# Lead growth over 36 steps, VectorE halves kept away from the sums of a, and h behind one eviction: a planner's rules changed in an attention-then-SwiGLU kernel

## The chip, the cores and the metric

The kernel runs on one core of a Trainium2 chip. The metric is device time in microseconds (us), the median of several runs. One profiled execution gives all rows that are quoted. Engines are named as the profile names them: PE (matrix multiplies; PEld is its weight loads), DVE (VectorE), ACT (ScalarE), POOL (GpSimd), SP (which issues the DMAs).

## The reference, cut to what matters

The input x has 4 batches of 12416 rows of 128 numbers. 32 inducing vectors attend to x and give h, the rows of x attend to h, and every resulting row goes through a gated feed-forward layer of width 1536.

```python
def mab(q, kv):
    s = scale * (q @ kv.transpose(0, 2, 1))
    a = np.exp(s - s.max(-1, keepdims=True))
    a /= a.sum(-1, keepdims=True) + 1e-09
    return a @ kv
h = mab(I, x)                  # (4, 32, 128)
x = mab(x, h)                  # (4, 12416, 128)
g = x @ w_gate; val = x @ w_val
out = (g / (1 + np.exp(-g)) * val) @ w_out
```

## The kernel before, in words

**What is multiplied.** Of each batch the second attention gives a (12416 x 32) only. The product of h with the gate and value weights is formed once a batch, so the feed-forward layer starts from a: its "stack" holds a in two parts (a_hi and a_lo, each 32 rows deep, stacked to a depth of 128). A batch's columns are cut in 25 pieces (COLS) of 512 or 480 rows of x, and each piece passes through 12 tiles of the width 1536: 300 slots a batch.

**One step of the wide part.** From the 13th piece of batch 0 on, two tiles go together (a pair, two slots). `fronts` (L910) issues four matmuls, the gates g of both tiles and the values v of both tiles. `gates` (L920) puts g through Silu on ACT. `values` (L927) forms h from v and the Silu on DVE. `splits` rounds h to fp16 (h_hi, a cast on ACT, L935) and subtracts (h_lo, on POOL, L937). `back` issues three matmuls for each tile (L954, L955, L956) into an accumulator o that gathers 12 tiles (t = 0 to 11). After t = 11 `evac` (L964) moves it out on DVE. `splits` of a pair is issued one pair later than its `values`.

**The lead.** Between `fronts` and `back` of a tile lie several other tiles, the lead (`ahead`, L1067): 8 tiles, and up to 14 while the next batch's first attention is being prepared. It grows by size / RAMP a slot, where size is 2 in the wide part and RAMP is 6, so by 6 tiles in 18 slots; while it grows, some pairs issue the backs of one tile only. At two places a batch, the bursts (the exponentials of the next batch's two attentions, here called e1 and e2), ACT has other work for long, and the lead falls back to 8: PE runs many backs at once.

**PSUM.** Six of the eight banks are three tiles of two banks (ps_two): g of a pair takes one, v the next, in turn. So g of a pair gets the tile that held v of the pair two before, which `values` must have read; v gets that of g of the pair before, which `gates` must have read. The other two banks are ps_o: the accumulator o, and whatever else needs a bank: the sums for the next batch's h (`hacc`, L442), its turning (`h_c`, L508), score visits, and the halves below.

**VectorE's halves.** Where `owned` (L972) says so, a pair is "own": DVE forms its h in two calls, one of them into a ps_o bank, and DVE itself casts and subtracts this half (L935 and L937 with o as operand), so that ACT and POOL have half the work on that pair. 130 of 522 pairs are own. Each needs one of the two ps_o banks until DVE's subtraction, so the next accumulator may have to wait for it.

**What sets the order.** The order on every engine is the order in which the kernel issues. Each batch has a list of steps with due slots (`plan`, `post`), which are issued between the tiles. `post` turns the raw exponentials into a piece of the stack: `sum2` (sum over the 32, two reductions on DVE), `rec2` (reciprocal), `scale2` (ACT), `norm2` (POOL), `aT` (a transpose on DVE), `a_hi` (DVE), `a_lo` (POOL). Steps with `acc` need a ps_o bank and are put off while the oldest waiting tile has t = 11, 0 or 1.

Of the kernel before, what the change touches and what calls it, by code (L numbers as in the profile page):

```python
# [38 lines left out]
NT = DFF // P  # L39
# [7 lines left out]
RAMP = 6  # L47
# [16 lines left out]
OWN = range(1, 7)  # L64
# [48 lines left out]
def induced_set_attention_then_swiglu(ctx: ExitStack, tc: tile.TileContext, xt, xn, ind, wgv, wo, out):  # L113
# [183 lines left out]
        nc.vector.tensor_reduce(out=pair[:, :, 0], in_=in_, op=ALU.add, axis=AX.X)  # L297
        nc.vector.tensor_reduce(out=out, in_=pair, op=ALU.add, axis=AX.X)

    keep = []  # L300

    class Batch:
        pass
# [1 line left out]
    def attention(b, one, xn0=None, xt0=None):  # L305
# [128 lines left out]
        def hacc(q, group):  # L434

            n0, n1 = CH0[group[0]], CH0[group[1]] + CH[group[1]]
            if q == group[0]:
                st.hps = ps_o.tile([P, 512], F32, name="o")
            for i in range(CH[q]):
                tb = CH0[q] + i - n0  # L440
                g = tb % NG
                nc.tensor.matmul(  # L442
                    out=st.hps[32 * g:32 * g + 32, 0:C], lhsT=st.eT[q][:, 32 * i:32 * i + 32], rhs=st.xn[q][:, i, :],
                    start=(tb < NG), stop=(tb >= n1 - n0 - NG))
            if q == group[1] and group[1] < NCH - 1:
                if group[0] == 0:
                    st.hn = att.tile([P, C], F32, name="hn")
                    nc.vector.tensor_copy(out=st.hn, in_=st.hps[:, 0:C])
                else:
                    nc.vector.tensor_add(out=st.hn, in0=st.hn, in1=st.hps[:, 0:C])  # L450

        def h_a():
            ps = bank()
# [6 lines left out]

        def h_b():
            nc.vector.tensor_add(out=st.hn, in0=st.hn, in1=st.hps[:, 0:C])
            nc.vector.tensor_scalar(out=st.hn, in0=st.hn, scalar1=st.r, scalar2=None, op0=ALU.mult)


# [253 lines left out]
    def post(st, q, eng, base, ready=0):  # L719

        f = st.f
        at = (1, 6, 7, 11, 13, 15, 18) if f["half"](q) else (1, 2, 2, 5, 7, 9, 12)
        steps = [(0, lambda: f["sum2"](q)), (at[0], lambda: f["rec2"](q)), (at[1], lambda: f["scale2"](q)), (at[2], lambda: f["norm2"](q, eng)),
                 (at[3], lambda: f["aT"](q)), (at[4], lambda: f["a_hi"](q)), (at[5], lambda: f["a_lo"](q, eng))]
        tiles = [u for u, (p, j) in enumerate(COLS) if p == q]
        return [(base + d, g) for d, g in steps] + [
            (max(base + at[6], ready + NT * (u - NST + 1) + 3), lambda u=u: f["spread"](u)) for u in tiles]
# [76 lines left out]
    with tc.tile_pool(name="xt0", bufs=NCH - NXT) as xt0, tc.tile_pool(name="xn0", bufs=NCH - NXN) as xn0:  # L804
        cur = attention(0, one, xn0, xt0)
        f = cur.f
# [16 lines left out]
        def run(token):  # L823
# [17 lines left out]
            at=f["aT"], ah=lambda q, e=0: f["a_hi"](q, (f["same"], nc.scalar.copy)[e]),  # L841
# [75 lines left out]
    def gates(u):  # L917
        u.s = twin(sip.tile([P, 2 * WF], F32, name="silu"), u)
        for f in halves if u.last else whole:
            nc.scalar.activation(out=f(u.s), in_=f(u.g), func=AF.Silu, scale=u.st.g)  # L920

    def values(u):
        u.h = twin(hp.tile([P, 2 * WF], F32, name="h"), u)
        u.x = ps_o.tile([P, 512], F32, name="o")[:, :u.n] if u.own else None
        u.parts = [(f, u.x if u.own and f is halves[1] else f(u.h)) for f in (halves if u.own else whole)]
        for f, h in u.parts:
            nc.vector.scalar_tensor_tensor(out=h, in0=f(u.v), scalar=u.st.k, in1=f(u.s), op0=ALU.mult, op1=ALU.mult)  # L927
# [13 lines left out]
    acc = {}  # L941
# [28 lines left out]
    quiet = {"own": 0, "step": 0}  # L970

    def owned(slot, burst):  # L972

        soon = [f for a in (cur, nxt) if a is not None for at, f in a.steps if at <= slot + 5]
        ok = not burst and pend and pend[0].t in OWN and slot >= max(quiet.values()) and not any(hasattr(f, "acc") and f.acc for f in soon)
        if ok:
            quiet["own"] = slot + 2 * REST
        return ok

    def parts(u):  # L980
        (splits if u.half else split)(u)

    pend, wait = [], []
# [13 lines left out]
    ahead = len(pend)  # L997
    for b in range(B):
        nxt = attention(b + 1, (one, oneb)[(b + 1) % 2]) if b + 1 < B else None
        if nxt is not None:  # L1000
            nxt.steps = plan(nxt, PA if b == 0 else PB, b + 1)
            if b == 0:
                cur.steps.append((nxt.e1, lambda: run(f"e2:52:{NTB}")))
                for q in range(2, NF):
                    base = NT * (1 + NG * (q - 1) - NST) + 2
                    base = max(base, E0 + 4) if q < 4 else max(base, nxt.e1 + 1)
                    cur.steps += post(cur, q, nc.gpsimd, base)
                cur.steps += [(14 + 6 * i, lambda i=i: peak_of(0, i)) for i in range(6)]
                cur.steps += [(66 + 6 * i, lambda i=i: peak_of(1, i)) for i in range(3)]
                small = [lambda f=f, k=k: f(k) for k in range(2) for f in (peak_a, peak_m, peak_b)] + [peak_c, peak_d]  # L1010
                sizes = [cur.f["size_" + k] for k in "abcdu"]
                small[2].acc = small[5].acc = sizes[1].acc = (NT - 1, 0, 1)
                cur.steps += list(zip((48, 53, 58, 84, 88, 94, 98, 101), small)) + list(zip((62, 68, 78, 82, 108), sizes)) + [(97, cur.f["proj_rounds"])]
                for k in range(2 * NG * NG):
                    cur.steps.append((100 + k // 2, lambda k=k: cur.f["proj_spread"](k // (NG * NG), k // NG % NG, k % NG)))
                cur.steps += [(106 + 6 * i, lambda i=i: (half_a, half_b, half_c)[i % 3](i // 3)) for i in range(9)]
                cur.steps.sort(key=lambda x: x[0])
        bursts = (nxt.bursts if nxt is not None else set()) | ({E0} if b == 0 else set())
        last_burst = max(bursts, default=0)
        slot2 = NT if b == 0 else 0  # L1020
        while slot2 < SLOTS:
            turn = b == 0 and slot2 == NT * CSW
            if turn:
                single.close()
                ps_two = ctx.enter_context(tc.tile_pool(name="ps_two", bufs=3, space=bass.MemoryType.PSUM))
            size = 1 if ps_two is None else 2
            top_, low_ = ((HI, SKEW), (HI2, SKEW2))[size - 1]
            c, t = slot2 // NT, slot2 % NT
            slots = range(slot2, slot2 + size)
            burst = any(x in bursts for x in slots)  # L1030
            if size == 1:
                u = front(cur, b, c, t)
                u.us = [u]
                u.last = False
                u.cast_dve = burst or t in CAST
                gate(u)
                value(u)
            else:
                if turn:
                    back(pend.pop(0))  # L1040
                u = fronts(cur, b, c, t)
                u.last = b == B - 1 and slot2 == SLOTS - 2
                u.cast_dve = burst
                u.own = u.last or owned(slot2, burst)
                gates(u)
                values(u)
            if wait:
                parts(wait[0])
                pend += wait.pop(0).us
            wait.append(u)  # L1050
            if burst:
                parts(u)
                pend += wait.pop(0).us
            def steps(slot):
                for a in (cur, nxt):
                    while a is not None and a.steps and a.steps[0][0] <= slot:

                        if pend and pend[0].t in getattr(a.steps[0][1], "acc", ()):
                            break
                        if getattr(a.steps[0][1], "acc", ()):  # L1060
                            quiet["step"] = slot + 8
                        a.steps.pop(0)[1]()

            for slot in slots:
                if size == 1:
                    steps(slot)
                ahead = min(ahead + size / RAMP, top_) if nxt is not None and slot < last_burst else max(ahead - 1 / RAMP, low_)  # L1067
                if slot in bursts:
                    ahead = low_ - (size == 1)
                while len(pend) + sum(len(x.us) for x in wait) > ahead + (slot != slots[-1]):  # L1070
                    back(pend.pop(0))
                if size == 2:
                    steps(slot)
            slot2 += size
        quiet = {k: at - SLOTS for k, at in quiet.items()}
        if nxt is not None:
            nxt.steps = [(at - SLOTS, f) for at, f in nxt.steps]
        cur = nxt
# [42 lines left out]
```

## Time and profile before

| what | value |
|---|---|
| median of 3 runs | 1409.54 us (1409.5 to 1410.22) |
| the profiled execution's own time | 1409.94 us |
| its span in the trace | 1408.1 us |
| granted PE clock | 0.999 |
| busy share of the span | PE 99%, ACT 86%, POOL 84%, DVE 83% |

Matmuls are pipelined: a row's duration has a tail that lies over the next matmul. The time a matmul takes from PE is the distance from its start to the next one's start, and a wait shows as a longer distance. The idle time that a row prints in brackets is what is left after the tail, some 0.16 us less than the time lost.

### The profile page before, as it was taken

Reading aid. Unit: us, or ns where it says so; the run is one execution under the profiler, and the core shown is the slowest. Engines: PE = TensorE matmul, PEld = TensorE weight load, DVE = VectorE, ACT = ScalarE, POOL = GpSimd, SP = SyncE. Lnnn points to the kernel's source line nnn. Section 1 sums busy time; section 2 is a strip of 40 time slices with the busy share of each in tenths; the row PEclk is TensorE's granted clock in tenths of the full one; section 3 lists DMA queues with packets and bytes.
Section 4 is the critical chain, followed back from the end, with each engine's and each line's share of the span. In section 5 each row is a group of like instructions: output and inputs, shape, how many; then the busy total and the mean of one; then the engine's idle time right before and its main releaser. Section 6 shows DMA issues by size and latency. Waiting matters only on the chain.

```text
span 1408.1 us, 21950 instructions
## 1 busy us (share of the span) xinstructions
PE 1388.9 (99%) x7480; PEld 706.4 (50%) x7480; DVE 1174.0 (83%) x1639; ACT 1209.3 (86%) x1481; POOL 1182.8 (84%) x748
## 2 busy tenths in 40 slices
PE   8999999999999999999999999999999999999998
PEld 6577687444444454444444444444444444444444
DVE  6889878879888777888898777779888889889887
ACT  4988798888898898888889888888888888888887
POOL 1679778998898888988889888988889888888887
PEclk9999999999999999999999999999999999999999
DMA  9224433211132432110103323211011010010010
GB/s 374 75 76 148 166 100 108 99 34 45 32 102 85 163 126 86 46 51 29 32 29 115 138 98 130 100 39 46 24 36 33 31 34 27 31 37 29 22 35 29
DMA packets 52335, 107.03 MB, mean 76 GB/s; under 512 B 13440, under 2 KB 34432, under 8 KB 52224
## 3 DMA queue, kind: packets, MB, share of 16 engines
q1 hardware_dynamic: 52224, 105.64, 22.2%
q8 instruction: 59, 0.97, 0.3%
q14 instruction: 52, 0.43, 0.1%
HBM read 62.87 MB, written 25.43 MB: 63 GB/s over the span
## 4 chain that ended last, share of the span: by engine, by line
PE 76%; DVE 9%; ACT 8%; issue 3%; SPq 1%; DMA 1%; POOL 0%; DVEq 0%; ACTq 0%
PE gw L910 24%; PE o L954 14%; PE o L955 14%; PE o L956 14%; DVE h L927 4%; ACT silu L920 4%; PE gv L870 2%; PE gv L869 2%; ACT h_hi L935 1%; DVE h_hi L935 1%; PE o L442 1%; PE o L369 1%; PE gw L369 1%; PE gv L369 1%; DVE o L927 1%
## 5 line engine op out<-in xcount | busy, mean ns | idle before, releaser
L937 POOL TENSOR_TENSOR h_lo<-h,h_hi 128x960 f16<-128x960 f32 (+2 forms) x522 | 949.3, 1836 | 142.9 <-ACT h_hi L935 139.3
L927 DVE SCALAR_TENSOR_TENSOR h<-gw,sc,silu 128x960 f32<-128x960 f32 (+2 forms) x522 | 580.7, 1113 | 162.5 <-ACT silu L920 144.4
L920 ACT ACTIVATE silu<-gw,sc 128x960 f32<-128x960 f32 (+2 forms) x523 | 566.3, 1083 | 125.5 <-PE gw L910 50.1
L935 ACT CAST h_hi<-h 128x960 f16<-128x960 f32 (+3 forms) x517 | 468.0, 905 | 12.4 <-DVE h L927 10.7
L954 PE MATMUL o<-h_hi,work 128*128 128x480 f16 (+1 forms) x1044 | 388.1, 372 | 2.9 <-DVE h_lo L937 2.1
L956 PE MATMUL o<-h_lo,work 128*128 128x480 f16 (+1 forms) x1044 | 388.1, 372 | 0.0
L955 PE MATMUL o<-h_hi,work 128*128 128x480 f16 (+1 forms) x1044 | 388.1, 372 | 0.0
L910 PE MATMUL gw<-stack,tw 128*128 128x512 f16 (+1 forms) x1200 | 301.3, 373 | 1.6 <-ACT silu L920 0.9
L910 PE MATMUL gw<-stack,work 128*128 128x480 f16 (+1 forms) x888 | 221.8, 371 | 2.2 <-ACT silu L920 0.9
L910 PEld LDWEIGHTS <-tw 128*128 128x128 f16 x1200 | 116.7, 98 | 139.5 <-issue 9.1
L893 POOL TENSOR_TENSOR h_lo<-h,h_hi 128x512 fp32r<-128x512 f32 x108 | 139.3, 1312 | 33.9 <-ACT h_hi L891 24.1
L955 PEld LDWEIGHTS <-work 128*128 128x128 f16 x1044 | 102.1, 98 | 120.6 <-issue 8.6
L954 PEld LDWEIGHTS <-work 128*128 128x128 f16 x1044 | 102.4, 98 | 117.8 <-issue 3.2
L956 PEld LDWEIGHTS <-work 128*128 128x128 f16 x1044 | 102.1, 98 | 115.5
L910 PEld LDWEIGHTS <-work 128*128 128x128 f16 x888 | 85.5, 98 | 105.9 <-issue 13.5
L875 ACT ACTIVATE silu<-gv 128x512 f32<-128x512 f32 x156 | 93.7, 603 | 15.4 <-PE gv L869 12.3
L927 DVE SCALAR_TENSOR_TENSOR o<-gw,sc,silu 128x480 f32<-128x480 f32 (+1 forms) x130 | 94.5, 727 | 0.0
L937 DVE TENSOR_TENSOR h_lo<-o,h_hi 128x480 f16<-128x480 f32 (+1 forms) x130 | 86.9, 669 | 4.5
L883 DVE TENSOR_TENSOR h<-gv,silu 128x512 f32<-128x512 f32 x108 | 73.2, 683 | 18.2 <-ACT silu L875 9.1
L935 DVE CAST h_hi<-o 128x480 f16<-128x480 f32 (+1 forms) x130 | 85.6, 658 | 0.0
L869 PE MATMUL gv<-stack,tw 128*128 128x512 f32 x156 | 65.5, 420 | 2.2 <-ACT silu L875 1.2
L891 ACT CAST h_hi<-h 128x512 fp32r<-128x512 f32 x95 | 58.9, 620 | 8.1 <-DVE h L883 7.4
(217 smaller groups left out, 1111.0 us busy)
## 6 DMA issues: line engine op xcount, KB each, us to landing
xt_sb<-xt SPq DMA_DIRECT2D x32, 896.0 KB, 4.9
xn_sb<-xn SPq DMA_DIRECT2D x18, 896.0 KB, 5.3
out<-ob SPq DMA_DIRECT2D x52, 256.0 KB, 2.0
out<-ob SPq DMA_DIRECT2D x48, 240.0 KB, 2.0
xt_sb<-xt SPq DMA_DIRECT2D x4, 832.0 KB, 5.5
stack<-a_hi SPq DMA_DIRECT2D x96, 30.0 KB, 1.8
stack<-a_lo SPq DMA_DIRECT2D x96, 30.0 KB, 1.8
xn_sb<-xn SPq DMA_DIRECT2D x3, 832.0 KB, 4.9
```

Of the source, the lines that this page charges most:

```text
L869: nc.tensor.matmul(out=u.g[:, :n], lhsT=st.w[:, wcol(0, t)], rhs=rhs, start=True, stop=True)
L875: nc.scalar.activation(out=u.s[:, :u.n], in_=u.g[:, :u.n], func=AF.Silu)
L883: nc.vector.tensor_mul(out=u.h[:, :n], in0=u.v[:, :n], in1=u.s[:, :n])
L893: eng.tensor_sub(out=u.lo[:, :n], in0=u.h[:, :n], in1=u.hi[:, :n].bitcast(F32))
L910: nc.tensor.matmul(out=x[:, 512 * (u.t - t):][:, :u.n], lhsT=st.wn[:, wcol(k, u.t)], rhs=st.stack[c][:, :u.n], start=True, stop=True)
L920: nc.scalar.activation(out=f(u.s), in_=f(u.g), func=AF.Silu, scale=u.st.g)
L927: nc.vector.scalar_tensor_tensor(out=h, in0=f(u.v), scalar=u.st.k, in1=f(u.s), op0=ALU.mult, op1=ALU.mult)
L935: (nc.vector.tensor_copy if h is u.x else one_wide if u.cast_dve else nc.scalar.copy)(out=f(u.hi), in_=h)
L937: (nc.vector if h is u.x else nc.gpsimd).tensor_sub(out=f(u.lo), in0=h, in1=f(u.hi))
L954: nc.tensor.matmul(out=o[:, :n], lhsT=w_lo[:, ws], rhs=u.hi[:, :n], start=(t == 0), stop=False)
L955: nc.tensor.matmul(out=o[:, :n], lhsT=w_hi[:, ws], rhs=u.hi[:, :n], start=False, stop=False)
L956: nc.tensor.matmul(out=o[:, :n], lhsT=w_hi[:, ws], rhs=u.lo[:, :n], start=False, stop=(t == NT - 1))
```

## The change

There are five edits; all of them move instructions or change which engine does a half, and PE's work stays the same.

1. For the batches after the first, the lead grows by 1 / RAMP a slot, 6 tiles in 36 slots.
2. `sum2` and `aT` carry a mark, and `owned` says no where such a step is due from one slot before to three slots after.
3. Where the pair ahead of a burst is own, its `parts` are issued before the burst pair's `gates` and `values`.
4. A list `open_` says that `hacc`'s sum (x's sum) holds a ps_o bank. While it does, and the oldest waiting tile has t of 10 or 11, `values` and the steps are issued behind the backs, so that `evac` stands ahead of `values` on DVE.
5. The number of own pairs follows from edits 1 and 2: 96 instead of 130.

```diff
@@ hacc: sum opened at its first piece, closed when DVE has read it (h_b too) @@
                 st.hps = ps_o.tile([P, 512], F32, name="o")
+                open_.append(b)
...
                     nc.vector.tensor_add(out=st.hn, in0=st.hn, in1=st.hps[:, 0:C])
+                del open_[:]
@@ post @@
+        for i in (0, 4):
+            steps[i][1].dve = True
@@ owned @@
-        ok = not burst and pend and pend[0].t in OWN and slot >= max(quiet.values()) and not any(hasattr(f, "acc") and f.acc for f in soon)
+        ok = not burst and pend and pend[0].t in OWN and slot >= max(quiet.values()) and not any(getattr(f, "dve", 0) for a in (cur, nxt) if a is not None for at, f in a.steps if slot - 1 <= at <= slot + 3) and not any(hasattr(f, "acc") and f.acc for f in soon)
@@ the loop over slots @@
                 u.own = u.last or owned(slot2, burst)
+                if burst and wait and wait[0].own:
+                    parts(wait[0])
+                    pend += wait.pop(0).us
                 gates(u)
-                values(u)
+                late = open_ and not burst and pend and pend[0].t >= NT - 2
+                if not late:
+                    values(u)
...
-                ahead = min(ahead + size / RAMP, top_) if nxt is not None and slot < last_burst else max(ahead - 1 / RAMP, low_)
+                ahead = min(ahead + (1 if b else size) / RAMP, top_) if nxt is not None and slot < last_burst else max(ahead - 1 / RAMP, low_)
...
-                if size == 2:
+                if size == 2 and not late:
+                    steps(slot)
+            if size == 2 and late:
+                values(u)
+                for slot in slots:
                     steps(slot)
```

What this moves, in the words of the built programs (lines of the changed kernel stand some 5 lower in the file: L932, L940, L942, L969 and L636 there are L927, L935, L937, L964 and L633 here).

First, DVE around the sum of a for a piece of batch 1 (slots 168 to 180). An own pair has two L927 rows, one into o, and later a CAST and a subtraction from o. Before:

```order
L927 SCALAR_TENSOR_TENSOR o<-gw,sc,silu 128x480
L297 TENSOR_REDUCE pairs<-s_all 128x15
L298 TENSOR_REDUCE sm<-pairs 128x15
L621 RECIPROCAL sm<-sm 128x15
L927 SCALAR_TENSOR_TENSOR h<-gw,sc,silu 128x2x480
L935 CAST h_hi<-o 128x480
L937 TENSOR_TENSOR h_lo<-o,h_hi 128x480
L927 SCALAR_TENSOR_TENSOR h<-gw,sc,silu 128x2x480
L964 TENSOR_SCALAR ob<-o,sc 128x480
L927 SCALAR_TENSOR_TENSOR h<-gw,sc,silu 128x2x480
L927 SCALAR_TENSOR_TENSOR h<-gw,sc,silu 128x480
L927 SCALAR_TENSOR_TENSOR o<-gw,sc,silu 128x480
```

And of the change:

```order
L932 SCALAR_TENSOR_TENSOR h<-gw,sc,silu 128x2x480
L297 TENSOR_REDUCE pairs<-s_all 128x15
L298 TENSOR_REDUCE sm<-pairs 128x15
L624 RECIPROCAL sm<-sm 128x15
L932 SCALAR_TENSOR_TENSOR h<-gw,sc,silu 128x2x480 x2
L969 TENSOR_SCALAR ob<-o,sc 128x480
L932 SCALAR_TENSOR_TENSOR h<-gw,sc,silu 128x2x480 x3
L636 STREAM_TRANSPOSE aT<-s_all 128x480
L932 SCALAR_TENSOR_TENSOR h<-gw,sc,silu 128x480
L932 SCALAR_TENSOR_TENSOR o<-gw,sc,silu 128x480
```

The halves at slots 170 and 178 are gone; the one at slot 182, right behind the transpose, stays.

Second, DVE at the burst e2 of batch 1 (slot 152 is own, slot 154 is the burst pair, whose cast is L930 before and L935 in the change). Before:

```order
L927 SCALAR_TENSOR_TENSOR o<-gw,sc,silu 128x512
L927 SCALAR_TENSOR_TENSOR h<-gw,sc,silu 128x1024
L935 CAST h_hi<-o 128x512
L937 TENSOR_TENSOR h_lo<-o,h_hi 128x512
L930 TENSOR_REDUCE h_hi<-h 128x1024
L964 TENSOR_SCALAR ob<-o,sc 128x512
```

And of the change:

```order
L932 SCALAR_TENSOR_TENSOR o<-gw,sc,silu 128x512
L940 CAST h_hi<-o 128x512
L942 TENSOR_TENSOR h_lo<-o,h_hi 128x512
L932 SCALAR_TENSOR_TENSOR h<-gw,sc,silu 128x1024
L935 TENSOR_REDUCE h_hi<-h 128x1024
L969 TENSOR_SCALAR ob<-o,sc 128x512
```

The half's cast and subtraction stand ahead of the burst pair's h.

Third, PE in the second pair of batch 1 (slot 2), behind its four front matmuls. Before:

```order
L954 LDWEIGHTS work
L954 MATMUL o<-h_hi,work 128x480
L955 LDWEIGHTS work
L955 MATMUL o<-h_hi,work 128x480
L956 LDWEIGHTS work
L956 MATMUL o<-h_lo,work 128x480
L910 LDWEIGHTS tw
L910 MATMUL gw<-stack,tw 128x512
```

And of the change:

```order
L959 LDWEIGHTS work
L959 MATMUL o<-h_hi,work 128x480
L960 LDWEIGHTS work
L960 MATMUL o<-h_hi,work 128x480
L961 LDWEIGHTS work
L961 MATMUL o<-h_lo,work 128x480
L959 LDWEIGHTS work
L959 MATMUL o<-h_hi,work 128x480
L960 LDWEIGHTS work
L960 MATMUL o<-h_hi,work 128x480
L961 LDWEIGHTS work
L961 MATMUL o<-h_lo,work 128x480
```

This pair issues the backs of two tiles instead of one. In the 18 slots in which the lead grew before, pairs issued 1.33 tiles on average; in the change it is 1.67 over 36 slots. The own pairs of the first 40 slots of batches 1 and 2 are at 2, 14, 18, 28, 32, 40 before, and at 2, 10, 14, 28, 40 in the change. `late` comes true once in batch 1 and once in batch 2, at slot 106.

More of the change, by code (lines that the diff above doesn't have):

```diff
@@ L298, in total @@
         nc.vector.tensor_reduce(out=out, in_=pair, op=ALU.add, axis=AX.X)
-    keep = []
+    keep, open_ = [], []
     class Batch:
@@ L462, in h_b @@
             nc.vector.tensor_add(out=st.hn, in0=st.hn, in1=st.hps[:, 0:C])
+            del open_[:]
             nc.vector.tensor_scalar(out=st.hn, in0=st.hn, scalar1=st.r, scalar2=None, op0=ALU.mult)
```

## The prediction

> **What bounds the kernel now.** I read the page first, then PE's timeline wherever the distance between two matmul starts is longer than the usual one, then DVE's, ACT's and POOL's timelines at those places.
>
> ```profile
> PE 1388.9 (99%) x7480; PEld 706.4 (50%) x7480; DVE 1174.0 (83%) x1639; ACT 1209.3 (86%) x1481; POOL 1182.8 (84%) x748
> ```
>
> PE bounds the whole, and the change leaves its matmuls alone. So it can win only what PE waits for. By start distances the repeated waits of the wide part are of four kinds. The first stands ahead of an accumulator's first matmul:
>
> ```profile
> 324.59 0.97 PE L910 MATMUL gw<-stack,work 128*128 128x480 f16 x4
> 325.83 0.36 PE L954 MATMUL o<-h_hi,work 128*128 128x480 f16 x1 [0.27 <-DVE h_lo L937]
> ```
> ```profile
> 321.94 0.65 DVE L297 TENSOR_REDUCE pairs<-s_all 128x15 f32<-128x480 f32 x1
> 322.62 0.18 DVE L298 TENSOR_REDUCE sm<-pairs 128x15 f32<-128x30 f32 x1
> 322.84 0.25 DVE L621 RECIPROCAL sm<-sm 128x15 f32<-128x15 f32 x1
> ...
> 325.12 0.66 DVE L937 TENSOR_TENSOR h_lo<-o,h_hi 128x480 f16<-128x480 f32 x1
> ```
>
> Four matmuls of 480 columns take 4 x (0.97 - 0.37) / 3 = 0.81 us of PE, so the next should start at 325.40; it starts at 325.83, 0.43 late. It waits for the bank that an own half holds until 325.12 + 0.66 = 325.78. That half is late because the sum of a and its reciprocal (321.94 to 323.09, 1.15 us) stand ahead of it. There are 22 such waits between L910 and L954, from this one to the last:
>
> ```profile
> 1334.19 0.97 PE L910 MATMUL gw<-stack,tw 128*128 128x480 f16 x4
> 1335.22 0.36 PE L954 MATMUL o<-h_hi,work 128*128 128x480 f16 x1
> ```
>
> This one loses 1335.22 - 1334.19 - 0.81 = 0.22. The 22 come to 3.8 us: 10 near a sum (1.2 us) and 12 behind a transpose of a (2.6 us, all but two of them of 0.22 to 0.29).
>
> The second kind comes where the lead grows:
>
> ```profile
> 407.40 0.37 PE L956 MATMUL o<-h_lo,work 128*128 128x480 f16 x1
> 408.45 1.02 PE L910 MATMUL gw<-stack,tw 128*128 128x512 f16 x4 [0.69 <-ACT silu L920]
> ...
> 419.84 1.03 PE L910 MATMUL gw<-stack,tw 128*128 128x512 f16 x4 [0.27 <-DVE o L927]
> ```
> ```profile
> 407.59 0.75 DVE L927 SCALAR_TENSOR_TENSOR o<-gw,sc,silu 128x512 f32<-128x512 f32 x1
> ```
>
> The matmul at 408.45 is due at 407.40 + 0.20: 0.85 late. It needs the tile that `values` of two pairs before reads until 408.34 (the row behind). Six waits from here to 419.84 come to 2.05 us in batch 1, and as much in batch 2. After e1 there are six more, 1.03 us in each of the two batches, from the first to the last of these rows (four matmuls without a wait are 1.03 long):
>
> ```profile
> 510.51 1.22 PE L910 MATMUL gw<-stack,tw 128*128 128x512 f16 x4
> ...
> 516.42 1.17 PE L910 MATMUL gw<-stack,tw 128*128 128x512 f16 x4
> ```
>
> The third kind is the burst e2:
>
> ```profile
> PE o L954 <- DVE h_lo L937: 2.1, 3, 0.9
> ```
> ```profile
> 590.53 0.38 PE L956 MATMUL o<-h_lo,work 128*128 128x512 f16 x1
> 591.85 0.38 PE L954 MATMUL o<-h_hi,work 128*128 128x512 f16 x1 [0.94 <-DVE h_lo L937]
> ```
> ```profile
> 588.05 0.75 DVE L927 SCALAR_TENSOR_TENSOR o<-gw,sc,silu 128x512 f32<-128x512 f32 x1
> 589.19 1.28 DVE L927 SCALAR_TENSOR_TENSOR h<-gw,sc,silu 128x1024 f32<-128x1024 f32 x1 [0.39 <-ACT silu L920]
> 590.39 0.68 DVE L935 CAST h_hi<-o 128x512 f16<-128x512 f32 x1
> 591.10 0.69 DVE L937 TENSOR_TENSOR h_lo<-o,h_hi 128x512 f16<-128x512 f32 x1
> ```
>
> 591.85 - 590.53 - 0.22 = 1.10 us. Of the three waits in the first row one is the 0.27 above; two of 0.94 remain, one for each burst e2: 2.2 us.
>
> The fourth is the turning of h:
>
> ```profile
> 534.72 0.38 PE L956 MATMUL o<-h_lo,work 128*128 128x512 f16 x1
> 535.40 0.49 PE L508 MATMUL o<-fold,hn 128*128 128x128 f32 x2 [0.30 <-DVE ob L964]
> ```
>
> 0.46 us, again in two batches: 0.9. All four kinds: 3.8 + 4.1 + 2.1 + 2.2 + 0.9 = 13.1 us.
>
> **The change part by part.** *Halves near sums.* At 325.8 the half at slot 218 is dropped, and its wait with it. At the transposes (2.6 us) the late half stays: it is issued right behind the transpose, which has left the list of steps by then. But the own pair two before it is dropped, and that one's cast and subtraction (0.65 + 0.66) no longer stand ahead of the transpose. The wait at 1335.22 is 0.22, so 1.3 us, or even half of that, clears it. I take 3.6 of 3.8; the bounds are 1.2 (the transposes' waits stay) and 3.8.
>
> What does it cost? 34 halves go back to ACT and POOL.
>
> ```profile
> 325.62 2.01 POOL L937 TENSOR_TENSOR h_lo<-h,h_hi 128x960 f16<-128x960 f32 x1 [1.36 <-ACT h_hi L935]
> ...
> 329.97 1.00 POOL L629 TENSOR_TENSOR s_all<-s_all,sm 128x480 f32<-128x480 f32 x1
> ```
> ```profile
> 329.87 0.37 PE L954 MATMUL o<-h_hi,work 128*128 128x480 f16 x1
> ```
>
> A whole pair takes POOL 2.01 us of a period of 10 x 0.2025 = 2.03. So without halves POOL just holds its pace, and `norm2` (1.00) puts it 1.0 behind until the next half. The pair done at 325.62 + 2.01 = 327.63 is used at 329.87: 2.2 us of room. I cost this at nothing; if that room were gone, each of the 34 would cost up to 1.0 (half of 2.01).
>
> *The slower lead.* What ACT needs for a pair:
>
> ```profile
> 418.17 1.04 ACT L935 CAST h_hi<-h 128x1024 f16<-128x1024 f32 x1
> 419.11 1.12 ACT L920 ACTIVATE silu<-gw,sc 128x1024 f32<-128x1024 f32 x1
> 420.11 0.62 ACT L935 CAST h_hi<-h 128x512 f16<-128x512 f32 x1
> 420.62 1.13 ACT L920 ACTIVATE silu<-gw,sc 128x1024 f32<-128x1024 f32 x1
> ```
>
> 0.94 for a cast and 1.00 for a Silu, start to start: 1.94, and 1.51 where a half is DVE's. PE needs 4 x 0.217 for the fronts and 3 x 0.217 for each tile's backs: with 1.33 tiles a pair 1.73 us, with 1.67 tiles 1.95. After e1, where no pair is own, 9 pairs at 1.73 leave ACT 9 x 0.21 = 1.9 short, of which 1.03 shows as waits and `hacc`'s PE time hides the rest. In the change ACT is short of nothing. I leave 0.3 for single pairs that issue one tile: 2 x 0.7 = 1.4 us won. At the batch's start the backs are of 480 columns at first and two pairs are own: ACT is short by about 9 x 0.25 - 2 x 0.43 = 1.4 of the 2.05, and the other 0.65 is DVE, which works off halves when `values` is due. That part stays, and grows: pairs 10 and 14 are own within the growth, and the sum at slot 26 falls into it. I leave 1.0: 2 x 1.05 = 2.1 us won. Bounds for both: nothing (ACT or DVE sets the pace at any slope) and 6.2.
>
> *The burst.* The half's cast and subtraction can follow 588.05 + 0.75 at once: 588.80 + 0.68 + 0.69 is 590.2, and the bank is due at 590.75. ACT casts its half ahead of the burst pair's Silu, which delays the exponentials by some 0.2; what is late next is the burst pair's h, 1.0 later, whose backs come after 10 others. I take all 2.2; the lower bound is 1.2, if that 1.0 stays on the path in one of the two batches.
>
> *h behind the eviction.* At slot 106 `values` waits behind the last backs and their eviction.
>
> ```profile
> 531.87 1.62 DVE L463 TENSOR_SCALAR hn<-hn,r 128x128 f32<-128x128 f32 x1
> 533.42 1.27 DVE L927 SCALAR_TENSOR_TENSOR h<-gw,sc,silu 128x1024 f32<-128x1024 f32 x1
> 534.61 0.74 DVE L964 TENSOR_SCALAR ob<-o,sc 128x512 f32<-128x512 f32 x1
> ```
> ```profile
> 531.28 4.29 POOL L937 TENSOR_TENSOR h_lo<-h,h_hi 128x1024 f16<-128x1024 f32 x2 [1.04 <-ACT h_hi L935]
> ```
> ```profile
> L463 DVE TENSOR_SCALAR hn<-hn,r x3: 286/1256/1625, 246.6 to 873.1; 128x128 f32<-128x128 f32 x3
> ```
>
> Without it the next accumulator, due right behind, would wait until `values` and the eviction are done, some 1.3 longer. With it, counted from the fronts of slot 106: the eviction runs from 1.75 to 2.5, the accumulator is due at 2.4 (0.2 late), `values` ends at 3.7, the scaling of h (0.29 to 1.62 in the rows) by 5.6, the turning is due at 5.4 (0.3 late), and the next `values`, behind it, ends at 6.8 where PE wants the tile at 6.6 (0.2 late). 0.7 instead of 0.46: 0.5 us lost in two batches; bounds 0.9 won and, should the scaling take a whole subtraction's 2.14 + 0.29, 2.2 lost.
>
> The scaling's three durations differ by who works beside it: the one of 1.62 ends at 533.49, as POOL's first subtraction ends (531.28 + 4.29 / 2 = 533.43). The Trainium skill (SBUF — State Buffer, Who interferes with whom) says that a DVE instruction in a two-port mode and a POOL instruction take the shared pair as an exclusive lock, so that the later one waits out the other. By that rule the scaling can wait out a whole subtraction, and the sum below would be 7.1 instead of 8.8. The row of 1.62 agrees with the rule.
>
> **The sum.** 3.6 + 2.1 + 1.4 + 2.2 - 0.5 = 8.8 us. The profiled execution took 1409.94 (span 1408.1), so 1401.1; the median of the runs is 0.4 below it: 1400.7.
>
> **The rivals.**
> - *The slope does not matter*: ACT or DVE sets the pace in the growth. For it: the waits are put down to ACT and DVE rows. Against: beyond the growth PE does not wait. 8.8 - 3.5 = 5.3: 1404.2.
> - *The marks do not do what they say*: the half behind each transpose stays late. 8.8 - 2.4 = 6.4: 1403.1.
> - *The scaling waits out POOL each time*, in the order that `late` makes: it takes 2.14 + 0.29 = 2.43 instead of 1.62, and the turning and the next `values` come 0.8 later in each batch. 8.8 - 1.7 = 7.1: 1402.4.
> - *POOL becomes the bound* (slower). Its 34 halves are 34 x 1.0 = 34 us more, at pairs where it already takes 2.01 of 2.03. For it: 1.0 of the 2.2 us of room goes to `norm2`, and `a_lo`, as long, follows. It decides once POOL is more than 2.2 behind; then 22 sums at 1.0 each cost 22: 1400.7 + 22 = 1423. Against: POOL waits for ACT ahead of 325.62 (1.36), so it is not behind there.
> - *No change*: what is won is spent on new bank waits of the same size. 1409.
>
> **How the numbers follow.** Forecast 0.55, slope 0.14, marks 0.12, scaling 0.10, POOL 0.04, no change 0.05. Low end: the sum's good bounds, 13.1 us, need everything at once; I go to 12, 1397.5. High end: the slope and the marks together, 8.8 - 3.5 - 2.4 = 2.9, come to 1406.6; one and a part of the other, 4.5 us, to 1405. The range 1397.5 to 1405 leaves out POOL, no change and the far ends of the others, under 0.2. A measurement tells about 0.2% (2.8 us) from no change: the first four cases lie below 1406.7, but for a tail. Faster 0.90, same 0.06, slower 0.04.
>
> **What would show it.** Right: no distance over 0.1 beyond the usual between L910's successor and L954's in the wide part; no wait of 0.94 at e2; fewer and shorter waits at 408 to 420 and 508 to 518; DVE's busy time down and POOL's up, with POOL still waiting for ACT. Wrong: PE waiting for POOL's h_lo, 0.2 us waits behind every transpose, or a new wait over 1 us at slots 106 to 112.

## The result, and the profile after

The changed kernel takes 1398.03 us (median of 6 runs, 1397.49 to 1399.3), the kernel before 1409.97 in the same comparison: a ratio of 0.9916 (95% interval 0.9903 to 0.9929), 11.9 us faster. The forecast was 1400.7, 8.8 us won on the profiled execution; the result lies 0.5 above the low end of the forecast range. All four kinds of waits shrank, and four of the five terms came out better than forecast. The profiled execution took 1397.54, 12.4 less than the one before; its span is 1395.8.

Lines have moved in the changed kernel: `fronts` is L915, `gates` L925, `values` L932, the cast L940, the subtraction L942, `back` L959 to L961, `evac` L969, the two steps of `h_b` L464 (sum) and L466 (scaling), the turning L511.

The page's row of busy times after:

```profile
PE 1381.9 (99%) x7480; PEld 705.4 (51%) x7480; DVE 1136.4 (81%) x1539; ACT 1221.3 (88%) x1481; POOL 1214.0 (87%) x748
```

PE does the same 7480 matmuls. DVE has 100 instructions and 38 us less, ACT has 12 us more and POOL 31: the 34 halves that went back. PE's busy sum fell by 7 for the same matmuls, because of each wait up to 0.16 counts as busy, the tail of the matmul ahead of it, and there are some 40 waits fewer. So this sum doesn't measure what was won; the distances between starts do.

*Near a sum of a.* PE's timeline, then DVE's:

```profile
324.23 0.97 PE L915 MATMUL gw<-stack,work 128*128 128x480 f16 x4
325.04 0.37 PE L959 MATMUL o<-h_hi,work 128*128 128x480 f16 x1
```
```profile
322.36 0.25 DVE L624 RECIPROCAL sm<-sm 128x15 f32<-128x15 f32 x1
322.52 1.15 DVE L932 SCALAR_TENSOR_TENSOR h<-gw,sc,silu 128x960 f32<-128x960 f32 x1
```

The accumulator's first matmul starts 0.81 after the fronts, which is what the four matmuls take; before it was 1.24. Behind the reciprocal stands a whole pair's h, and no half that would hold a bank.

*Behind a transpose.* DVE, then PE:

```profile
331.23 0.67 DVE L636 STREAM_TRANSPOSE aT<-s_all 128x480 f32<-128x480 f32 x1
...
335.90 0.66 DVE L942 TENSOR_TENSOR h_lo<-o,h_hi 128x480 f16<-128x480 f32 x1
```
```profile
336.38 0.97 PE L915 MATMUL gw<-stack,work 128*128 128x480 f16 x4
337.19 0.37 PE L959 MATMUL o<-h_hi,work 128*128 128x480 f16 x1
```

The half behind the transpose is still there, as forecast, but it frees its bank at 336.56, 0.63 before the accumulator is due. All 22 waits between L915 and L959 are gone.

*Where the lead grows*, PE again:

```profile
407.21 0.37 PE L961 MATMUL o<-h_lo,work 128*128 128x480 f16 x1
407.41 1.03 PE L915 MATMUL gw<-stack,tw 128*128 128x512 f16 x4
...
432.14 0.38 PE L961 MATMUL o<-h_lo,work 128*128 128x512 f16 x1
432.58 1.02 PE L915 MATMUL gw<-stack,tw 128*128 128x512 f16 x4
```

The wait of 0.85 at the first place is gone (0.20 from start to start). What stays is 0.08 at 411, 0.13 at 422 and 0.23 at 432.58 (0.44 less the 0.21 of one matmul): 0.44 in a batch, where it was 2.05. After e1 the groups of four are 1.03 long, without a wait, as in this row:

```profile
514.46 1.03 PE L915 MATMUL gw<-stack,tw 128*128 128x512 f16 x4
```

*The burst e2.* DVE, then PE:

```profile
584.49 0.69 DVE L940 CAST h_hi<-o 128x512 f16<-128x512 f32 x1
585.22 0.69 DVE L942 TENSOR_TENSOR h_lo<-o,h_hi 128x512 f16<-128x512 f32 x1
585.83 1.27 DVE L932 SCALAR_TENSOR_TENSOR h<-gw,sc,silu 128x1024 f32<-128x1024 f32 x1
```
```profile
586.18 0.38 PE L961 MATMUL o<-h_lo,work 128*128 128x512 f16 x1
586.40 0.38 PE L959 MATMUL o<-h_hi,work 128*128 128x512 f16 x1
```

The half's cast and subtraction stand ahead of the burst pair's h, and the bank is free at 585.22 + 0.69 = 585.91, ahead of the accumulator's start at 586.40. The backs run on at 0.21 or 0.22 from start to start: the wait of 1.10 is gone. The burst pair's h comes 1.0 later than before against PE's backs (3.36 earlier by the clock of the trace, where the backs are 590.75 - 586.40 = 4.35 earlier), and it is not waited for.

*The turning of h.* PE, DVE and POOL:

```profile
527.92 1.03 PE L915 MATMUL gw<-stack,tw 128*128 128x512 f16 x4
528.93 0.38 PE L959 MATMUL o<-h_hi,work 128*128 128x512 f16 x1
...
531.52 0.38 PE L961 MATMUL o<-h_lo,work 128*128 128x512 f16 x1
531.74 0.38 PE L511 MATMUL o<-fold,hn 128*128 128x128 f32 x2
...
534.20 1.18 PE L915 MATMUL gw<-stack,tw 128*128 128x512 f16 x4
```
```profile
528.13 0.75 DVE L969 TENSOR_SCALAR ob<-o,sc 128x512 f32<-128x512 f32 x1 [0.45 <-PE o L961]
528.80 1.27 DVE L932 SCALAR_TENSOR_TENSOR h<-gw,sc,silu 128x1024 f32<-128x1024 f32 x1
...
530.30 1.15 DVE L466 TENSOR_SCALAR hn<-hn,r 128x128 f32<-128x128 f32 x1
```
```profile
529.23 4.23 POOL L942 TENSOR_TENSOR h_lo<-h,h_hi 128x1024 f16<-128x1024 f32 x2 [1.37 <-ACT h_hi L940]
```

The accumulator waits 0.14 for the eviction (528.93 - 527.92 - 0.87), the turning not at all (0.22 behind the back before it), and the fronts behind the late `values` 0.09 and 0.15 (the last row is 1.18 long in place of 1.03): 0.38 in a batch, against 0.46 before.

By kind, in the waits of the wide part: sums and transposes 3.8 won, the start of the batches 2 x 1.6 = 3.2, after e1 2 x 1.03 = 2.1, the burst 2.2, the turning 0.2: 11.5 of the 12.4 us between the two profiled executions. Of the rest 0.37 lies ahead of the wide part, which no edit touches; the other 0.5 is spread over waits of 0.12 and less.

### The profile page after: what moved, and what is told of

Same layout as the page of the kernel before. It is cut to its first block, busy times and chain, and to the rows that moved or that the text cites. A ratio compares the mean times of both kernels' runs of the same rounds, so it can differ in the third digit from the quotient of the medians.

```text
span 1395.8 us, 21858 instructions
## 1 busy us (share of the span) xinstructions
PE 1381.9 (99%) x7480; PEld 705.4 (51%) x7480; DVE 1136.4 (81%) x1539; ACT 1221.3 (88%) x1481; POOL 1214.0 (87%) x748
## 4 chain that ended last, share of the span: by engine, by line
PE 90%; ACT 5%; DMA 2%; DVE 1%; issue 1%; SPq 0%; DVEq 0%; ACTq 0%
PE gw L915 30%; PE o L959 17%; PE o L960 17%; PE o L961 17%; PE gv L875 2%; PE gv L874 2%; PE o L443 1%; PE o L369 1%; PE gw L369 1%; DMA s_all<-wgv 1%; ACT silu L925 1%; ACT silu L880 1%; DMA xt<-xt 1%; ACT h_hi L896 1%; PE o L956 1%
## 5 line engine op out<-in xcount | busy, mean ns | idle before, releaser
L942 POOL TENSOR_TENSOR h_lo<-h,h_hi 128x960 f16<-128x960 f32 (+1 forms) x522 | 980.6, 1899 | 100.4 <-ACT h_hi L940 96.7
L932 DVE SCALAR_TENSOR_TENSOR h<-gw,sc,silu 128x960 f32<-128x960 f32 (+3 forms) x524 | 601.3, 1148 | 190.6 <-ACT silu L925 179.3
L925 ACT ACTIVATE silu<-gw,sc 128x960 f32<-128x960 f32 (+2 forms) x523 | 567.2, 1085 | 114.9 <-PE gw L915 46.4
L940 ACT CAST h_hi<-h 128x960 f16<-128x960 f32 (+3 forms) x517 | 481.7, 932 | 2.0 <-DVE h L932 1.6
L959 PE MATMUL o<-h_hi,work 128*128 128x480 f16 (+1 forms) x1044 | 388.2, 372 | 0.0
L961 PE MATMUL o<-h_lo,work 128*128 128x480 f16 (+1 forms) x1044 | 388.2, 372 | 0.0
L915 PE MATMUL gw<-stack,tw 128*128 128x512 f16 (+1 forms) x1200 | 300.6, 373 | 0.3
L915 PE MATMUL gw<-stack,work 128*128 128x480 f16 (+1 forms) x888 | 221.2, 371 | 0.9 <-DVE r L459 0.4
L915 PEld LDWEIGHTS <-tw 128*128 128x128 f16 x1200 | 116.8, 98 | 137.0 <-issue 5.3
L959 PEld LDWEIGHTS <-work 128*128 128x128 f16 x1044 | 102.3, 98 | 117.9 <-issue 3.6
L961 PEld LDWEIGHTS <-work 128*128 128x128 f16 x1044 | 102.1, 98 | 115.5
L915 PEld LDWEIGHTS <-work 128*128 128x128 f16 x888 | 85.5, 98 | 103.6 <-issue 10.1
L932 DVE SCALAR_TENSOR_TENSOR o<-gw,sc,silu 128x480 f32<-128x480 f32 (+1 forms) x96 | 69.9, 728 | 0.0
L942 DVE TENSOR_TENSOR h_lo<-o,h_hi 128x480 f16<-128x480 f32 (+1 forms) x96 | 64.3, 670 | 3.3
L969 DVE TENSOR_SCALAR ob<-o,sc 128x480 f32<-128x480 f32 (+1 forms) x87 | 62.9, 723 | 3.9 <-PE o L961 3.9
```

The lines of the kernel that those rows point to most:

```text
L915: nc.tensor.matmul(out=x[:, 512 * (u.t - t):][:, :u.n], lhsT=st.wn[:, wcol(k, u.t)], rhs=st.stack[c][:, :u.n], start=True, stop=True)
L940: (nc.vector.tensor_copy if h is u.x else one_wide if u.cast_dve else nc.scalar.copy)(out=f(u.hi), in_=h)
L942: (nc.vector if h is u.x else nc.gpsimd).tensor_sub(out=f(u.lo), in0=h, in1=f(u.hi))
L959: nc.tensor.matmul(out=o[:, :n], lhsT=w_lo[:, ws], rhs=u.hi[:, :n], start=(t == 0), stop=False)
L961: nc.tensor.matmul(out=o[:, :n], lhsT=w_hi[:, ws], rhs=u.lo[:, :n], start=False, stop=(t == NT - 1))
```

## The experiments

**The theory:** PE waits only for ps_o banks that DVE holds and for tiles that ACT and DVE read too late, each edit takes away the waits of its own kind, and the halves given back cost nothing. **Its rivals:** (a) the edits depend on each other, so that the slope alone does little or the marks alone do; (b) the gain comes from the smaller number of halves, or POOL is at its limit and eats a part of it. Runs 1 to 4 undo one edit each and run 6 undoes half of edit 2, runs 5 and 12 make one edit alone in the kernel before, the others vary a size or go further.

Each run was compared with the kernel before anew, and the median of that kernel lay between 1409.65 and 1410.42. So what a run lost or won against the changed kernel is given here as the difference of what the two won against their own before (11.9 for the changed kernel). The interval of a ratio reaches some 1.8 us to either side. Where two versions differ by less than about 2 us, it is the waits in their traces that show the difference, and not the medians.

**1. The old slope, all else as changed** (98 own pairs).

```diff
-(1 if b else size) / RAMP
+size / RAMP
```

> The changed kernel with the lead growing in 18 slots again. If the edits act each on its own waits, the waits of the growth come back: 1.6 us at the start and 1.0 us after e1 in each of batches 1 and 2, and the turning of h waits 0.46 instead of 0.38: 5.4 us more than the changed kernel, 1403.4. If the slope does not matter and the marks or the burst edit freed VectorE there, it stays at 1398 to 1399. The waits near sums and at e2 stay away in both cases.

Measured: 1404.1 us, ratio to before 0.9953 (0.9939 to 0.9966). PE at the first place of the growth:

```profile
406.62 0.37 PE L961 MATMUL o<-h_lo,work 128*128 128x480 f16 x1
407.68 1.02 PE L915 MATMUL gw<-stack,tw 128*128 128x512 f16 x4 [0.69 <-ACT silu L925]
```

The wait of 0.86 is back (407.68 - 406.62 - 0.20), and with it the other five (2.06 a batch) and the six after e1 (1.03): 2 x (1.62 + 1.03) and 2 x 0.08 at the turning of h, 5.5 us. 5.6 us lost (6.3 won against 1410.42): the slope matters, and the rival that ACT or DVE sets the pace at any slope is out.

**2. The marks taken out of `owned`** (130 own pairs again).

```diff
-... and not any(getattr(f, "dve", 0) ... if slot - 1 <= at <= slot + 3) and not any(hasattr(f, "acc") ...
+... and not any(hasattr(f, "acc") ...
```

> The changed kernel without the marks on the sum and the transpose: 130 own pairs instead of 96. If the halves near the sums caused the 22 waits ahead of an accumulator, they come back, 3.8 us, and the growth gets a little worse by the half at slot 24: 1402 to 1402.5. If the waits went because of the other edits, it stays at 1398; if the 34 halves are worth more to ScalarE and GpSimd than the waits cost, it is below 1398.

Measured: 1403.51, ratio 0.9948 (0.9935 to 0.996). The 22 waits between L915 and L959 are back, 3.8 us in all, and there is something new within the longer growth:

```profile
433.71 0.38 PE L961 MATMUL o<-h_lo,work 128*128 128x512 f16 x1
434.27 0.59 PE L915 MATMUL gw<-stack,tw 128*128 128x512 f16 x2 [0.18 <-ACT silu L925]
435.48 0.59 PE L915 MATMUL gw<-stack,tw 128*128 128x512 f16 x2 [0.61 <-DVE o L932]
```

A sum of a with an own half on either side of it costs 0.35 and 0.78 here (434.27 - 433.71 - 0.22, and 435.48 - 434.27 - 0.43): 1.12 in a batch in place of the 0.23 at 432.58. So beside the new slope the marks are worth 3.8 + 2 x 0.89 = 5.6 us by the waits (5.0 by the medians: 6.9 won against 1410.42), not only the 3.8 of the waits that they were read from.

**3. The burst pair's order as before.**

```diff
-if burst and wait and wait[0].own:
+if False:
```

> The changed kernel without the parts ahead of the burst. The wait of 1.1 us ahead of the accumulator at e2 comes back in batches 1 and 2 and nothing else: 2.2 us more, 1400.2. If the marks had already freed VectorE at e2, it stays at 1398.

Measured: 1400.02, ratio 0.9923 (0.9911 to 0.9936): 1.5 us lost (10.4 won against 1410.42). The row of the wait is back, once in each of two batches, 1.10 by start distances each time:

```profile
588.01 0.38 PE L959 MATMUL o<-h_hi,work 128*128 128x512 f16 x1 [0.94 <-DVE h_lo L942]
```

**4. `late` never true**, so h stands ahead of the eviction as before.

```diff
+late = False
```

> The changed kernel with values always ahead of the backs. At slot 106 the eviction stands behind values, so the next accumulator starts 1.2 us later in batches 1 and 2, and the turning of h no longer waits behind it: 2.0 to 2.4 us more, 1400 to 1400.4. If the order there does not matter, because h_b holds the bank anyway, it stays within 0.3 us of 1398.

Measured: 1400.74, ratio 0.9929 (0.9916 to 0.9941). PE and DVE:

```profile
528.35 1.03 PE L915 MATMUL gw<-stack,tw 128*128 128x512 f16 x4
530.73 0.38 PE L959 MATMUL o<-h_hi,work 128*128 128x512 f16 x1 [1.35 <-DVE ob L969]
```
```profile
528.73 1.28 DVE L932 SCALAR_TENSOR_TENSOR h<-gw,sc,silu 128x1024 f32<-128x1024 f32 x1 [1.81 <-ACT silu L925]
```

The accumulator waits 1.52 (530.73 - 528.35 - 0.86) for an eviction that stands on DVE behind this h. In the kernel before this place cost only 0.46. With the slower growth the lead stands elsewhere when x's sum is turned, and the tile's end falls on `values`. So edit 4 wins little against before (0.2), and 2 x (1.52 - 0.38) = 2.3 against the new slope without it, as much as the medians show (9.7 won against 1410.42, 2.3 lost): it repairs what edit 1 breaks.

**5. The slope alone,** in the kernel before.

```diff
-size / RAMP
+(1 if b else size) / RAMP
```

> The kernel before with the slower lead alone. If the edits were independent, the growth's gain of 5.3 us would show alone: 1404.9. If the slower lead needs the others, less: the half at slot 24 (which the marks forbid) costs 0.9 us in each of batches 1 and 2, and the accumulator at slot 106 waits 1.5 us in each, against 0.46 less at the turning of h: 5.3 - 1.8 - 3.0 + 0.9 = 1.4 us faster than before, 1408.8.

Measured: 1408.09, ratio 0.9987 (0.9978 to 0.9996): 1.9 us won of the 5.6 that it brings in company. PE at the two places that take the rest:

```profile
435.23 0.59 PE L910 MATMUL gw<-stack,tw 128*128 128x512 f16 x2 [0.62 <-DVE o L927]
...
532.32 0.38 PE L954 MATMUL o<-h_hi,work 128*128 128x512 f16 x1 [1.35 <-DVE ob L964]
```

The waits of run 2 (1.12 in a batch) and of run 4 (1.52 in place of 0.46) stand here together, and 0.2 of the growth's own: 6.2 - 2 x (1.12 + 1.06 + 0.2) = 1.4, where 1.9 was measured. Rival (a) holds for the slope: it pays in full only together with the marks and `late`.

**6. The mark on the sum alone,** none on the transpose (112 own pairs).

```diff
-for i in (0, 4):
+for i in (0,):
```

> The changed kernel with the mark on the sum alone, 112 own pairs. If the half issued ahead of a transpose is what made the half behind it late, the ten waits of 0.22 to 0.29 behind transposes come back and the ones near sums do not: 2.4 us more, 1400.4. If the transposes' waits went through the sums' mark, it stays at 1398.

Measured: 1400.43, ratio 0.9932 (0.9919 to 0.9944): 2.4 us lost. PE and DVE:

```profile
336.87 0.97 PE L915 MATMUL gw<-stack,work 128*128 128x480 f16 x4
337.86 0.36 PE L959 MATMUL o<-h_hi,work 128*128 128x480 f16 x1
```
```profile
332.40 0.66 DVE L942 TENSOR_TENSOR h_lo<-o,h_hi 128x480 f16<-128x480 f32 x1
332.97 0.67 DVE L636 STREAM_TRANSPOSE aT<-s_all 128x480 f32<-128x480 f32 x1
...
337.15 0.66 DVE L942 TENSOR_TENSOR h_lo<-o,h_hi 128x480 f16<-128x480 f32 x1
```

With the pair ahead of the transpose own again, its subtraction stands in front of the transpose, and the half behind ends at 337.81, 0.13 after the accumulator is due (336.87 + 0.81 = 337.68), where in the changed kernel it ended 0.63 ahead. The accumulator waits 0.18. Twelve such waits of 0.08 to 0.25 are back, 2.2 us in all, those near the sums are not. That is the step by which the prediction had the second mark work, and it speaks against the mere number of halves as the cause: the waits come back only where the halves did. No run takes away as many halves in other places.

**7. No halves at all** (`OWN` empty; only the very last pair keeps its own).

```diff
+OWN = ()
```

> The changed kernel without own pairs (but the last). A stretch of 24 pairs then takes GpSimd 24 x 2.01 + 2.1 = 50.3 us against 48.6 of TensorE's. If GpSimd is near its limit, as the bound rival had it, the room of 2.2 us is used up within two stretches and each further one costs 1.7: some 12 stretches, 15 to 25 us more, 1413 to 1423. If its pace has room, it stays within 1 us of 1398.

Measured: 1407.43, ratio 0.9983 (0.9974 to 0.9992), 9.4 us slower than the changed kernel: a miss, between the two cases that I had set. The page's row, and the two largest waits of PE in the wide part:

```profile
PE 1385.6 (99%) x7480; PEld 707.0 (50%) x7480; DVE 1017.9 (72%) x1254; ACT 1258.4 (90%) x1481; POOL 1294.8 (92%) x748
```
```profile
PE o L961 <- POOL h_lo L942: 4.1, 9, 0.7
PE gw L915 <- DVE h L932: 3.3, 2, 1.6
```

The second of them in the timelines of PE, DVE and POOL:

```profile
445.47 0.59 PE L915 MATMUL gw<-stack,tw 128*128 128x512 f16 x2 [1.64 <-DVE h L932]
```
```profile
443.54 0.71 DVE L636 STREAM_TRANSPOSE aT<-s_all 128x512 f32<-128x512 f32 x1 [2.23 <-POOL s_all L632]
444.18 1.24 DVE L932 SCALAR_TENSOR_TENSOR h<-gw,sc,silu 128x1024 f32<-128x1024 f32 x1
```
```profile
442.44 1.07 POOL L632 TENSOR_TENSOR s_all<-s_all,sm 128x512 f32<-128x512 f32 x1
```

POOL runs without a pause around these rows, so `norm2` comes late; DVE waits 2.23 for it with the transpose, `values` stands behind that, and PE's fronts wait for `values` (444.18 + 1.24 = 445.42), 1.80 by start distances. The same wait of 1.8 comes once more, in batch 2, and in eleven other places PE waits ahead of L961, which reads POOL's low part (0.24 to 0.86 at a time, 6.1 in all): 9.7 us together. The 95 halves are worth 9.4 us, about 0.1 each, and not the 1.0 that a half takes. POOL falls behind slowly and catches up where PE has the next batch's attention to do as well: in the wide part of this trace it pauses for ACT before 312, from 480 to 605 and from 819 to 944, and nowhere else. So rival (b) holds in this far: without any halves PE would wait for POOL. It doesn't with 96, where POOL still waits for ACT (the 1.37 in the row of 529.23).

**8. The scaling reads PSUM:** the sum is written back into x's sum in its bank, and the scaling takes it from there.

```diff
-nc.vector.tensor_add(out=st.hn, in0=st.hn, in1=st.hps[:, 0:C])
-nc.vector.tensor_scalar(out=st.hn, in0=st.hn, scalar1=st.r, ...)
+nc.vector.tensor_add(out=st.hps[:, 0:C], in0=st.hn, in1=st.hps[:, 0:C])
+nc.vector.tensor_scalar(out=st.hn, in0=st.hps[:, 0:C], scalar1=st.r, ...)
```

> The changed kernel with the sum of h left in its PSUM bank, so that the scaling reads PSUM instead of SBUF. If the scaling waited for a port that it shares with GpSimd, it takes 0.3 us instead of 1.15, the next values end 0.85 earlier, and the two waits of 0.09 and 0.15 at slots 110 to 114 go: 0.4 to 0.5 us less in both batches together, 1397.6. If the 1.15 has another cause, its duration stays above 1.

Measured: 1397.11 (4 runs), ratio 0.9909 (0.9896 to 0.9923). DVE and POOL:

```profile
529.83 0.35 DVE L466 TENSOR_SCALAR hn<-o,r 128x128 f32<-128x128 f32 x1
```
```profile
528.75 8.43 POOL L942 TENSOR_TENSOR h_lo<-h,h_hi 128x1024 f16<-128x1024 f32 x4 [1.19 <-ACT h_hi L940]
```

POOL subtracts from 528.75 on, and the scaling in its midst takes 0.35 instead of 1.15. The waits of 0.09 and 0.15 are gone, 0.5 us in two batches. This is the fastest version measured, but its interval overlaps the changed kernel's; that it is faster is shown by the trace's waits, not by the runs.

**9 and 10. Other slopes:** growth over 27 and over 54 slots.

```diff
-(1 if b else size) / RAMP
+(4 / 3 if b else size) / RAMP
+(2 / 3 if b else size) / RAMP
```

> The changed kernel with the lead growing over 27 slots in batches 1 and 2 (1.5 tiles a pair). If what counts is that TensorE's pair (1.84 us there) must not be shorter than ScalarE's (1.94), 13.5 pairs are short of 0.1 each, 1.4 us per growth less what the halves and the sums for h hide: waits of 0.3 to 0.8 in each growth, and the turning of h waits behind an eviction again, 0.5: 1 to 2.5 us more than 1398.0. If any slope below 18 slots will do, it stays at 1398.

> The changed kernel with the lead growing over 54 slots (1.78 tiles a pair, 2.02 us of TensorE against 1.94). If the balance with ScalarE decides, nothing is short: the waits of 0.44 in the first growth go to about 0.2, but the sums for h come 4 slots later, behind an accumulator's first tiles, with h_b and h_c right behind them, which may cost 0.5 each: within 1 us of 1398.0. If a slower growth leaves the lead too short for the burst, waits appear at e2.

Measured: 1402.69, ratio 0.9949 (0.9937 to 0.9962) for 27, and 1399.61, ratio 0.9926 (0.9914 to 0.9939) for 54. Both are slower than I expected. The waits in batch 1, with PE's time for a pair by the prediction's 4 x 0.217 for fronts and 3 x 0.217 for each tile's backs (ACT needs 1.94; at 27 slots a pair issues 2 - 12/27 = 1.56 tiles, not the 1.5 behind the 1.84 above):

| growth over | PE a pair | start of batch | after e1 | turning of h | time |
|---|---|---|---|---|---|
| 18 slots (run 1) | 1.73 | 2.06 | 1.03 | 0.46 | 1404.1 |
| 27 (run 9) | 1.88 | 1.37 | 0.14 | 1.36 | 1402.69 |
| 36 (changed) | 1.95 | 0.44 | none | 0.38 | 1398.03 |
| 54 (run 10) | 2.03 | 0.17 | none | 0.56 | 1399.61 |

The columns for the start of the batch and after e1 fall as PE's time for a pair comes up to ACT's 1.94 and passes it, which is how the prediction had it. What I had left out is the last column. At 27 slots the eviction stands behind the scaling and a `values`, between them 531.26 to 532.53 (PE, then DVE):

```profile
531.66 0.38 PE L961 MATMUL o<-h_lo,work 128*128 128x512 f16 x1
533.24 0.49 PE L511 MATMUL o<-fold,hn 128*128 128x128 f32 x2 [1.20 <-DVE ob L969]
```
```profile
529.46 1.88 DVE L466 TENSOR_SCALAR hn<-hn,r 128x128 f32<-128x128 f32 x1
...
532.45 0.73 DVE L969 TENSOR_SCALAR ob<-o,sc 128x512 f32<-128x512 f32 x1
```

At 54 slots the turning waits 0.56 for the scaling, and two of the attention's steps and one behind the turning wait longer too (0.13, 0.29 and 0.22 in batch 1; the 0.29 is put down to an eviction, the other two stay open). So 36 is the best of four not by its growth, where 54 is better by 0.27 a batch, but by where the tiles' ends meet the turning. Against 54 that rests on these waits: the intervals of the two runs overlap.

**11. Run 8, and no own pair within four slots behind a sum,** against the wait at 432.58, where an own half and the sum fall together.

```diff
+quiet["sum"] = slot + 4      # when a sum is issued
```

> The changed kernel with the sum of h left in PSUM for the scaling, and no own pair within 4 slots behind a sum of a, which moves the half at slot 28 to slot 30 in batches 1 and 2. The first saves 0.5 us as before; the wait of 0.23 at slot 32 should go with the half at 28, another 0.5: 1397.0. If the half at 30 only moves the wait, 1397.5.

Measured: 1397.77, ratio 0.9913 (0.9899 to 0.9926). PE (lines are one higher here):

```profile
438.47 0.38 PE L962 MATMUL o<-h_lo,work 128*128 128x512 f16 x1
438.99 1.02 PE L916 MATMUL gw<-stack,tw 128*128 128x512 f16 x4
```

The wait of 0.23 became one of 0.10, and a new one of 0.30 came six us later (438.99 - 438.47 - 0.22). It moved and did not go, which is the second of the two cases set.

**12. The marks alone,** in the kernel before (98 own pairs).

```diff
+for i in (0, 4):
+    steps[i][1].dve = True
...
+... and not any(getattr(f, "dve", 0) ... if slot - 1 <= at <= slot + 3) ...
```

> The kernel before with the rule on the VectorE half alone: none beside the sums of a, so 34 halves go back to ScalarE and GpSimd (98 left), with the slope over 18 slots, the pairs at a burst and the turning of h as before. If the 34 halves given back cost ScalarE and GpSimd nothing, the 22 waits around the sums and transposes go (3.8 us) and those of the growth (2 x 2.05), of the section after it (2 x 1.03), of the burst (2.2) and of the turning stay: 1410.1 - 3.8 = 1406.3. If each half costs about what one of the 96 cost when all were left out (0.1 us), waits of TensorE for the low part or for an h buffer appear at the ends of stretches and the time is 1408 to 1410. Then the slope, not the marks, would be what makes room for it.

Measured: 1406.07, ratio 0.9973 (0.9963 to 0.9984); before 1409.65 in this comparison. In the waits of PE, the group of the halves:

```profile
PE o L956 <- DVE h_lo L939: 1.9, 2, 0.9
```

Of the waits for a half only the two of the burst are left, the growth's are as they were, and there is none for POOL's low part. 3.6 us: the forecast's term for the marks, paid in full, and the 34 halves cost nothing even at the old slope. Rival (a) does not hold for the marks alone.

## Why the prediction was right, step by step

The mechanism held: PE waited for banks and tiles, and each edit took away the kind of wait that it was read from. The sizes were less good, and their errors lie on one side: the terms were 2.7 us too small together, and 0.9 of the 12.4 stood in no term. The sizes, as they stood in the sum:

| term | forecast | measured | shown by |
|---|---|---|---|
| halves near sums and transposes | 3.6 | 3.8 | run 12 alone: 3.6; run 6 for the transposes |
| growth at the start of a batch | 2.1 | 3.2 | waits of after; run 1 |
| growth after e1 | 1.4 | 2.1 | waits of after; run 1 |
| burst e2 | 2.2 | 2.2 | waits of after; run 3 |
| h behind the eviction | -0.5 | +0.2 | waits of after; run 4 |

- **The growth was mis-sized by 1.8 us.** Its step "I leave 1.0" at the start of a batch counted on DVE's halves staying in the way and on the sum at slot 26 falling into the longer growth; 0.44 was left. The sum does cost there, but run 2 shows what makes it cost: an own half on each side, 1.12 a batch. One of the two the marks take away, and the 1.0 has no term for that. After e1 "I leave 0.3" was caution with no row behind it; there was none.
- **The turning was mis-sized by 0.7 us.** The accumulator waited 0.14 (0.2 forecast), but the step that failed is the turning, "due at 5.4 (0.3 late)": it did not wait, because the scaling took 1.15, not 1.62 or more, and ended at 531.45, 0.29 before PE's turning at 531.74. The next `values` cost 0.09 and 0.15 in place of 0.2.
- **What edit 4 is for** the prediction had right: without it the accumulator would wait "some 1.3 longer", and run 4 shows 1.52 in place of 0.14, 1.38 longer. What its sum doesn't say is that this is a cost of edit 1. Before, the place cost 0.46; with the lead moved, a tile's end meets `values` just there. So the slope's terms, 2.1 + 1.4, are what it wins with edit 4 beside it, and not what it wins alone.
- **34 halves at nothing** was right (run 12), and the reason given, room for POOL, too: the pair whose low part POOL ends at 331.85 is used at 333.14. POOL as a bound is real but further off: with 129 halves gone it costs 9.4 us (run 7), with 34 nothing. The room did shrink as costed, from 2.2 to 1.29 behind a `norm2` of 1.0.
- **The rivals.** The slope matters (run 1), the marks do what they say (runs 6 and 12), POOL isn't the bound with 96 halves. The scaling does wait out POOL each time, but only for what is left of the subtraction that runs when it comes.

## What to carry over

Rules that shift a pipeline's phase are not to be costed one at a time: the slope alone won 1.9 us, in company 5.6, since it moves which tile's end meets which step. When work is balanced between engines, take the helper whose work frees what PE's next matmul needs, and compare its time for a unit with PE's time for the same unit (here ACT's 1.94 with 1.73, 1.88, 1.95 and 2.03), since the wait follows their difference. It need not be the helper that takes longest: POOL took 2.14 for a whole pair, but in the growth of the changed kernel its result lay ready 2.1 us or more before PE used it. Read waits as distances between starts, and look for the new place of a wait before a fix of it is counted as won.

## What the runs showed of the hardware

The scaling of 128 x 128 numbers took 0.29 with POOL idle, and 1.15, 1.62 and 1.88 with POOL subtracting. Each of these three ended within 0.1 of the end of POOL's running subtraction: before at 533.49 (the row of 1.62 in the prediction), in the changed kernel at 531.45 against 529.23 + 4.23 / 2 = 531.35, in run 9 at 531.34 against the half of POOL's two subtractions from 529.12 to 533.35, 531.24. Over all kernels here there are 24 such scalings, of 0.96 to 1.88, and each ended 0.08 or 0.09 after the subtraction that ran when it came. From PSUM the same step took 0.35, amid POOL's work (four times in runs 8 and 11) and with POOL idle alike. The Trainium skill (SBUF — State Buffer, Who interferes with whom) says that a DVE instruction in a two-port mode and POOL exclude each other on a shared pair of ports, and that one with at most one SBUF input outside these modes does not contend. These rows agree with both halves of it; the price is not a whole subtraction, but what is left of it.
